# A decode block on one core: the output stored in whole rows, the MLP weights loaded in other pieces, and the second bias loaded by itself

## The chip, the cores and the metric

The kernel runs on one core of a Trainium2 chip. The metric is the device time of one execution in microseconds, the median of several runs. The core's engines work side by side: TensorE (PE, its weight loads PEld), VectorE (DVE), ScalarE (ACT), GpSimd (POOL) and SyncE (SP). SP computes nothing here; it issues the loads and the store, each a DMA that sixteen DMA engines carry out.

## The reference

Four tokens (B = 4, one per sequence) of D = 448 go through an attention block over cached keys and values, and then through an MLP, each behind a layer norm and with its residual. All is float32.

```
x = A_x                                  # 4 x 1 x 448
q = layernorm(x) @ wq                    # 16 heads of 256
k, v = the last W = 1024 rows of k_cache, v_cache   # 8 kv heads, each for 2 heads
p = softmax(q k^T / 16)
h = x + (p v) @ wo                       # wo: 4096 x 448
y = layernorm(layernorm(h))
g = gelu(y @ w1 + b1)                    # w1: 448 x 1792
out = h + g @ w2 + b2                    # w2: 1792 x 448
```

Of the 88 MB that it reads, 67 MB are k and v, 4.2 MB of each for every kv head. The four weights are 21 MB, the biases next to nothing.

## The kernel before, in words

**Tiles and loads.** `block_kernel` goes over the eight kv heads g. For each it loads one block of k with the head's part of wq behind it (`load_k`), and one of v with its part of wo (`load_v`). All large loads are issued by SP and go to a ring of four slots, taken in turn (`slot`), so a load waits until the tile that had its slot is no longer read. In order: `first` (wq of head 0 and x), k0, k1, v0, k2, v1, and so on to k7, v6. Then, in the loop's last turn (lines 310 to 320): v7 in two parts (`load_v7`, line 91), wo of heads 6 and 7 in two loads (line 314), w1 in two (line 317), w2 in three of 8, 4 and 2 chunks (line 320; a chunk is 128 rows of w2 as 128 partitions x 448, 224 KB). wo of heads 6 and 7 and w1 share a slot.

**The small rows.** x, b2 and b1 stand in one tile `rs` of 128 x 704, cleared by POOL (line 133) and filled by one ACT-issued load `rows` (line 134). With four tokens and a row of 448 cut into four quadrants there are 16 rows, and row i stands on partition 8 i (GAP = 8); the rest stays zero. `xb`, `b2b` and `b1b` are its column ranges.

**Compute.** For each head: `scores` (line 184, then maximum and exp), `project_q` for the head two ahead, `transpose_p` (line 209), `values` (line 220, po), `heads` (lines 237 to 252, po to oT) and `project_o` (line 257 into acc; for the last two heads line 263 into hsum). Behind head 7: h = hsum + x (line 352), the means and variances by small matmuls on PE (line 343), z, zT (line 368), hb = h + b2 (line 370), pu = z w1 (line 379), u with b1 and gelu (lines 392, 393), the transposes put (398, 400) and gT (402, 404), py = g w2 (line 410, eight matmuls a chunk), res = py + hb (line 414) and the store (line 415), 16 rows of 512 bytes.

**What sets the order.** PE's instructions run as the file has them. On the other engines the planner may put an instruction ahead of an earlier one that is not ready. `keep_warm(n)` puts n matmuls of zeros on PE whose results are not used; PE's clock depends on how busy it is.

The host cuts and packs the inputs, and picks the 448 columns out of the 4 x 512 that the store leaves.

Of the kernel before, what the change touches and what calls it, by code (L numbers as in the profile page):

```python
# [8 lines left out]
F32 = mybir.dt.float32  # L9
# [6 lines left out]
B, D = 4, 448  # L16
HQ, HKV, SK, DH = 16, 8, 4096, 256
REP = HQ // HKV
W = min(4096, max(256, SK // 4))
F = 1792  # L20
P = 128
# [4 lines left out]
FQ = F // 4  # L26
Q = 32
GAP = Q // B
KV = 8 * B * DH
WC = 4 * D  # L30
# [3 lines left out]
W1C = 3 * F + F // 2  # L34
# [1 line left out]
SCALE = DH ** -0.5  # L36

@with_exitstack
def block_kernel(ctx: ExitStack, tc, rows, first, kw, vw, v7, wo67, w1, w2, out):
    nc = tc.nc  # L40
    const = ctx.enter_context(tc.tile_pool(name="const", bufs=1))
    ring = ctx.enter_context(tc.tile_pool(name="ring", bufs=4))
    work = ctx.enter_context(tc.tile_pool(name="work", bufs=2))
    once = ctx.enter_context(tc.tile_pool(name="once", bufs=1))
# [3 lines left out]
    ps_m = ctx.enter_context(tc.tile_pool(name="ps_m", bufs=2, space=PSUM))  # L48
# [4 lines left out]
    def slot(name):  # L53
        return ring.tile([P, SLOT], F32, tag="t", name=name)
# [17 lines left out]
    def wo_rows(t):  # L72
        return t.rearrange("p (j e) -> p j e", j=4)

    def load_k(g):
        t = load(kw[g] if g < HKV - 1 else kw[g][:, :KV], f"k{g}")
        k = t[:, :KV].rearrange("p (h c b k) -> p h c b k", h=2, c=2, b=B)
        return [k[:, h] for h in range(2)], wq_parts(t[:, KV:]) if g < HKV - 1 else None

    def chunk_pairs(t):  # L80
        t = t.rearrange("p (c b d) -> p c b d", c=NKC, b=B)
        return [t[:, c : c + 2] for c in range(0, NKC, 2)]

    def load_v(g):
        t = load(vw[g] if g < HKV - 2 else vw[g][:, :KV], f"v{g}")
        return chunk_pairs(t[:, :KV]), wo_rows(t[:, KV:]) if g < HKV - 2 else None

    def load_v7():
        t = slot("v7")
        for a, b in ((0, V7A), (V7A, KV)):  # L90
            nc.sync.dma_start(t[:, a:b], v7[:, a:b])
        return chunk_pairs(t[:, :KV])

# [35 lines left out]
    for t in qT + oT + pT + [gT]:  # L129
        nc.gpsimd.memset(t, 0.0)  # L130

    rs = const.tile([P, 2 * P + FQ], F32, name="rs")
    nc.gpsimd.memset(rs, 0.0)
    nc.scalar.dma_start(rs[::GAP, :], rows)

    def spread(t):
        return t[..., ::GAP]
    xb, b2b, b1b = rs[:, :P], rs[:, P : 2 * P], rs[:, 2 * P :]


    def column_mean(t, name):
# [19 lines left out]
    def project_q(g, parts):  # L161
        pq = ps_m.tile([P, 512], F32, tag="m", name=f"pq{g}")
        for j, a, cols, w in parts:
            nc.tensor.matmul(pq[j * Q : (j + 1) * Q, cols], yT[:, a, :], w, start=True, stop=True)  # L164
        qs = work.tile([P, 512], F32, tag="qs", name=f"qs{g}")
        nc.scalar.copy(qs, pq)  # L166

        pt = ps_m.tile([P, 2 * REP, B], F32, tag="m", name=f"pqt{g}")
        for i in range(2 * REP):
            nc.tensor.matmul(pt[:, i, :], qs[:, i * P : (i + 1) * P], sel[:, :B], start=True, stop=True)  # L170

        src = pt.rearrange("p (r c) b -> p c b r", r=REP)
        for i in range(2):
            nc.vector.tensor_copy(qT[g % 2][:, :, :, i * REP : (i + 1) * REP], src)  # L174

    def scores(g, kt):
        s = [ps_s.tile([P, 512], F32, tag="s", name=f"s{g}_{h}") for h in range(2)]
        if g == HKV - 1:
            keep_warm(12, s[0])
        mx = work.tile([P, 2], F32, tag="mx", name=f"mx{g}")  # L180
        for h in range(2):
            for c in range(2):
                for b in range(B):
                    nc.tensor.matmul(  # L184
                        s[h][b * Q : (b + 1) * Q, :], qT[g % 2][:, c, b, :], kt[h][:, c, b, :],
                        start=(c == 0), stop=(c == 1),
                    )
            nc.vector.reduce_max(mx[:, h : h + 1], s[h], axis=AX.X)  # L188
        nm = work.tile([P, 1], F32, tag="nm", name=f"nm{g}")
        nc.vector.tensor_max(nm, mx[:, 0:1], mx[:, 1:2])  # L190
        nc.vector.tensor_scalar_mul(nm, nm, -SCALE)  # L191
        p = work.tile([P, 2 * 512], F32, tag="p", name=f"p{g}")
        sums = work.tile([P, 2], F32, tag="sums", name=f"sums{g}")
        for h in range(2):
            nc.scalar.activation(  # L195
                p[:, h * 512 : (h + 1) * 512], s[h], AF.Exp, bias=nm, scale=SCALE,
                accum_out=sums[:, h : h + 1],
            )
        rec = work.tile([P, 1], F32, tag="rec", name=f"rec{g}")
        nc.vector.tensor_add(rec, sums[:, 0:1], sums[:, 1:2])  # L200
        nc.vector.reciprocal(rec, rec)
        return p, rec

    def transpose_p(g, p):
        pt = ps_t.tile([P, NKC, P], F32, tag="t", name=f"ppt{g}")
        if g == HKV - 1:
            keep_warm(8, pt.rearrange("p c k -> p (c k)"))
        for c in range(NKC):
            nc.tensor.transpose(pt[:, c, :], p[:, c * P : (c + 1) * P], ident)  # L209

        src = pt.rearrange("p (c i) (b q) -> p c i b q", i=2, b=B)
        for i in range(2):
            nc.vector.tensor_copy(pT[g % 2][:, :, :, i * REP : (i + 1) * REP], src[:, :, i, :, :REP])  # L213
# [16 lines left out]
    def columns(t, j):  # L230
        if j < 3:
            return t[:, j * P : (j + 1) * P].rearrange("p (i c) -> p i c", i=2)
        return t[:, None, 3 * P :].to_broadcast([t.shape[0], 2, H])
# [47 lines left out]
    def keep_warm(n, to=None):  # L281
        to = tail[0][:, 0, :] if to is None else to
        for _ in range(n):
            nc.tensor.matmul(to[:Q, :512], idle[:, :Q], idle, start=True, stop=True)  # L284
# [6 lines left out]
    for g in range(HKV):  # L291
        if g + 1 < HKV:
            kt, wqt = load_k(g + 1)
            vt, wot = load_v(g)
            p, rec_next = scores(g + 1, kt)
            if g + 2 < HKV:
                project_q(g + 2, wqt)
            transpose_p(g + 1, p)
            if g + 1 == HKV - 1:
                tail.append(ps_t.tile([P, 2, 512], F32, tag="t", name="tail"))  # L300
                accs = once.tile([P, D], F32, tag="u", name="accs")
                nc.scalar.copy(accs, acc)
                keep_warm(10)
                hsum = ps_s.tile([P, 512], F32, tag="s", name="hsum")[:, :P]
                ph = hsum.rearrange("p (i c) -> p i c", i=2)
                pu = ps_s.tile([P, 512], F32, tag="s", name="pu")[:, :FQ]
                for j in range(4):
                    nc.tensor.matmul(ph[j * Q : (j + 1) * Q], sel, columns(accs, j), start=True, stop=False)
        else:
            vt = load_v7()  # L310
            tw = slot("w1")
            wo_last = [wo_rows(tw[:, i * WC : (i + 1) * WC]) for i in range(2)]
            for i in range(2):
                nc.sync.dma_start(tw[:, i * WC : (i + 1) * WC], wo67[i])
            tw1 = tw[:, 2 * WC : 2 * WC + W1C]
            for a, n in ((0, 2 * F), (2 * F, W1C - 2 * F)):
                nc.sync.dma_start(tw1[:, a : a + n], w1[:, a : a + n])
            tw2 = slot("w2")
            for c0, n in ((0, 8), (8, 4), (12, 2)):
                nc.sync.dma_start(tw2[:, c0 * D : (c0 + n) * D], w2[:, c0 * D : (c0 + n) * D])  # L320
        po = values(g, vt)
        heads(g, po, rec)
        if g < HKV - 2:
            project_o(g, wot)
        if g == HKV - 1:
            for i in range(2):
                project_o(HKV - 2 + i, wo_last[i])
        if g + 1 < HKV:
            rec = rec_next
# [20 lines left out]
    h = once.tile([P, P], F32, tag="h", name="h")  # L350
# [3 lines left out]
    m = row_mean(hs, pm[:, 0:1], "m")  # L354
# [4 lines left out]
    m = row_mean(ds, pm2[:, 0:1], "m2")  # L359
# [6 lines left out]
    pz = ps_m.tile([P, 4, B], F32, tag="m", name="pz")  # L366
    nc.tensor.matmul(pz, z, rows_of, start=True, stop=True)
    nc.vector.tensor_copy(spread(zT), pz)
    hb = once.tile([P, P], F32, tag="hb", name="hb")
    nc.vector.tensor_add(hb, h, b2b)  # L370
    keep_warm(2)

    r1 = stat("r1")
# [2 lines left out]
    for a in range(ND):  # L376
        for j in range(4):
            rows, w = w1_part(a, j)
# [27 lines left out]
    for c in range(NFC):  # L406
        for j in range(4):
            n = 2 if c == 0 or j < 3 else 1
            w = columns(w2t[c], j) if n == 2 else w2t[c][:, None, 3 * P :]
            nc.tensor.matmul(  # L410
                py[j * Q : (j + 1) * Q, :n, :], gT[:, c, :], w, start=(c == 0), stop=(c == NFC - 1),
            )
    res = once.tile([P, P], F32, tag="res", name="res")
    nc.vector.tensor_add(res, py.rearrange("p i c -> p (i c)"), hb)  # L414
    nc.sync.dma_start(out, res[::GAP, :])


# [62 lines left out]
```

## Time and profile before

| | |
|---|---|
| median of 3 runs | 215.99 us |
| the three runs | 215.67, 215.99, 216.38 us |
| the profiled execution | 215.79 us |
| its span (first to last instruction) | 213.8 us |
| mean granted clock of TensorE | 0.83 |
| read from memory | 88.29 MB, 413 GB/s over the span |
| PE, DVE, ACT, POOL busy | 71%, 16%, 11%, 3% |

The span in forty slices, of 5.3 us each:

```profile
PE   0476868294786538495957768485948897999993
DMA  7999999999999999999999999999999999999990
```

A digit is the busy share of a slice in tenths. For DMA it is the mean over the sixteen DMA engines: they are full from the first slice to the last but one. PE is busy in turns, and full only in the last slices, in which the MLP runs.

In the rows that follow, a time in front is the start in us from the span's start, the next number the duration, x32 a count. SPq is SP's queue of DMA issues, whose duration is the issuing alone. A landing time runs from the issue to the end of the transfer. A bracket at the end of a row tells how long the engine stood idle before it and for what.

### The profile page before, as it was taken

What the parts mean: (1) busy time and instruction counts of PE and PEld (TensorE: products, weight loads), DVE (VectorE), ACT (ScalarE), POOL (GpSimd) and SP (SyncE); (2) the same over time, 40 slices, a digit from 0 to 9 for tenths busy, and PEclk for the clock granted to TensorE, in tenths of its full rate; (3) what the DMA queues carried; (4) which work ended last, traced back from release to release, by engine and by line L of the source; (5) the groups of instructions that cost most, each with busy time, mean ns of one, the idle gap of its engine ahead of it and who ended that gap; (6) DMA issues with size and microseconds to landing.
All of it is one profiled execution on the core that took longest, in us unless ns stands there. A gap on an engine that the chain in (4) does not pass through costs nothing.

```text
span 213.8 us, 2594 instructions
## 1 busy us (share of the span) xinstructions
PE 151.1 (71%) x1128; PEld 63.9 (30%) x1128; DVE 33.5 (16%) x138; ACT 24.0 (11%) x57; POOL 5.6 (3%) x17
## 2 busy tenths in 40 slices
PE   0476868294786538495957768485948897999993
PEld 0342423122142213222231213122232333456352
DVE  1410313101121103100130103100220113002220
ACT  1110302000030002100030003000030102000310
POOL 6100000000000000000000000000000000000100
PEclk9999978769589959766695859666795999999999
DMA  7999999999999999999999999999999999999990
GB/s 297 412 433 441 396 478 406 427 448 403 456 421 411 478 411 426 444 396 471 418 418 448 406 456 426 411 466 418 426 419 417 460 414 411 411 418 427 428 368 22
DMA packets 3674, 88.45 MB, mean 414 GB/s; under 512 B 432, under 2 KB 448, under 8 KB 1104
## 3 DMA queue, kind: packets, MB, share of 16 engines
q1 hardware_dynamic: 3632, 88.25, 96.6%
q8 instruction: 8, 0.13, 0.3%
q10 hardware_dynamic: 32, 0.05, 0.1%
q14 instruction: 2, 0.02, 0.0%
HBM read 88.29 MB, written 0.01 MB: 413 GB/s over the span
## 4 chain that ended last, share of the span: by engine, by line
DMA 83%; PE 12%; DVE 1%; ACT 1%; SPq 1%; issue 1%; ACTq 0%
DMA v<-vw 70%; DMA w<-w 13%; PE po L220 8%; PE acc L257 2%; PE pot L245 1%; PE py L410 1%; DVE o L237 1%; ACT o L238 1%; SPq L59 0%; DVE oT L252 0%; SPq L63 0%; DVE res L414 0%; ACTq L238 0%
## 5 line engine op out<-in xcount | busy, mean ns | idle before, releaser
L184 PE MATMUL s<-k,qT 128*32 128x512 f32 x256 | 42.6, 819 | 17.4 <-DMA k<-kw 17.4
L220 PE MATMUL po<-v,pT 128*32 128x512 f32 x256 | 40.9, 792 | 18.3 <-DMA v<-vw 18.3
L184 PEld LDWEIGHTS s<-k,qT 128*32 128x32 f32 x256 | 10.4, 144 | 48.5 <-issue 28.7
L220 PEld LDWEIGHTS po<-v,pT 128*32 128x32 f32 x256 | 11.1, 140 | 42.3 <-issue 26.7
L188 DVE TENSOR_REDUCE mx<-s 128x1 f32<-128x512 f32 x16 | 11.1, 692 | 64.8 <-PE s L184 64.8
L166 ACT COPY qs<-pq 128x512 f32<-128x512 f32 x8 | 4.7, 586 | 85.8 <-PE pq L164 85.8
L170 PE MATMUL pqt<-sel,qs 128*128 128x4 f32 x64 | 9.3, 268 | 6.2 <-ACT qs L166 6.2
L245 PE MATMUL pot<-ident,o 128*128 128x8 f32 x64 | 9.8, 261 | 4.9 <-DVE o L237 3.6
L237 DVE TENSOR_SCALAR o<-po,rec 128x256 f32<-128x256 f32 x8 | 3.9, 484 | 59.9 <-PE po L220 59.9
L238 ACT ACTIVATE o<-po,rec 128x256 f32<-128x256 f32 x8 | 3.8, 474 | 72.7 <-DVE o L237 72.7
L245 PEld LDWEIGHTS pot<-ident,o 128*128 128x128 f32 x64 | 8.3, 190 | 11.7 <-DVE o L237 9.7
L195 ACT ACTIVATE p<-s,nm 128x512 f32<-128x512 f32 x16 | 10.9, 690 | 7.0 <-DVE nm L191 7.0
L170 PEld LDWEIGHTS pqt<-sel,qs 128*128 128x128 f32 x64 | 8.6, 208 | 10.4 <-ACT qs L166 10.4
L209 PE MATMUL ppt<-ident,p 128*128 128x128 f32 x64 | 9.0, 281 | 0.7 <-ACT p L195 0.7
L257 PE MATMUL acc<-v,oT 128*32 128x448 f32 x48 | 8.0, 751 | 1.7 <-DVE oT L252 1.7
L209 PEld LDWEIGHTS ppt<-ident,p 128*128 128x128 f32 x64 | 7.3, 150 | 1.7 <-ACT p L195 1.4
L164 PE MATMUL pq<-k,yT 128*32 128x512 f32 (+1 forms) x70 | 7.3, 507 | 0.0
L284 PE MATMUL tail<-idle 128*32 128x512 bf16 x26 | 7.0, 382 | 0.4 <-DVE pT L213 0.4
L284 PEld LDWEIGHTS <-idle 128*32 128x32 bf16 x52 | 4.6, 96 | 7.9 <-issue 3.9
L158 POOL TENSOR_TENSOR r<-ve_r,mhalf 128x1 f32<-128x1 f32 x2 | 1.1, 545 | 192.2 <-DVE ve_r L157 192.2
L164 PEld LDWEIGHTS pq<-k,yT 128*32 128x32 f32 x70 | 3.3, 110 | 6.0 <-issue 4.6
L174 DVE COPY qT<-pqt 128x16 f32<-128x16 f32 x16 | 2.0, 170 | 15.5 <-PE pqt L170 15.5
(97 smaller groups left out, 66.3 us busy)
## 6 DMA issues: line engine op xcount, KB each, us to landing
k<-kw SPq DMA_DIRECT2D x7, 4992.0 KB, 41.3
v<-vw SPq DMA_DIRECT2D x6, 4992.0 KB, 39.3
k<-kw SPq DMA_DIRECT2D x1, 4096.0 KB, 39.1
v<-vw SPq DMA_DIRECT2D x1, 4096.0 KB, 32.9
w<-w SPq DMA_DIRECT2D x2, 1792.0 KB, 28.7
v<-v SPq DMA_DIRECT2D x1, 3072.0 KB, 32.3
w<-wo SPq DMA_DIRECT2D x2, 896.0 KB, 22.8
w<-w SPq DMA_DIRECT2D x1, 1344.0 KB, 30.3
```

What stands on the lines that cost most here:

```text
L164: nc.tensor.matmul(pq[j * Q : (j + 1) * Q, cols], yT[:, a, :], w, start=True, stop=True)
L170: nc.tensor.matmul(pt[:, i, :], qs[:, i * P : (i + 1) * P], sel[:, :B], start=True, stop=True)
L184: nc.tensor.matmul(s[h][b * Q : (b + 1) * Q, :], qT[g % 2][:, c, b, :], kt[h][:, c, b, :], start=(c == 0), stop=(c == 1),)
L188: nc.vector.reduce_max(mx[:, h : h + 1], s[h], axis=AX.X)
L195: nc.scalar.activation(p[:, h * 512 : (h + 1) * 512], s[h], AF.Exp, bias=nm, scale=SCALE, accum_out=sums[:, h : h + 1],)
L209: nc.tensor.transpose(pt[:, c, :], p[:, c * P : (c + 1) * P], ident)
L220: nc.tensor.matmul(po[b * Q : (b + 1) * Q], pT[g % 2][:, c, b, :], vt[c][:, :, b, :], start=(c == 0), stop=(c == NKC // 2 - 1),)
L237: nc.vector.tensor_scalar_mul(o[:, 0], po[:, 0], rec)
L238: nc.scalar.mul(o[:, 1], po[:, 1], rec)
L245: nc.tensor.matmul(pt[:, c], o[:, i, c * P : (c + 1) * P], rows_of_pair[:, i * REP : (i + 1) * REP, :], start=(i == 0), stop=(i == 1),)
L257: nc.tensor.matmul(acc[i * Q : (i + 1) * Q, :], oT[g % 2][:, i, :], wt[:, i, :], start=(g == 0), stop=(g == HKV - 3),)
L284: nc.tensor.matmul(to[:Q, :512], idle[:, :Q], idle, start=True, stop=True)
```

## The change

1. The store writes the whole tile `res`, 128 rows of 512 bytes, and the host takes every eighth row.
2. b2 is no longer in `rows`. It has a tile `b2b` of 128 x 128, cleared by POOL, and eight loads on SP: for each of the four 32-column parts, the 16 rows in two loads. Parts 0 and 1 (2 and 14 rows, 6 and 10 rows) stand between v7's two loads, parts 2 and 3 (4 and 12, 8 and 8) ahead of the last load of w2. A row of a part is 128 bytes.
3. wo of heads 6 and 7 comes in one load instead of two, w1 in three instead of two, w2 in four (8, 3, 2 and 1 chunks) instead of three.
4. hb = h + b2 stands behind the matmuls of py, ahead of res; before, it stood behind zT.
5. `keep_warm(8)` is added behind `transpose_p(6, p)`, ahead of `values(5)`.

```diff
+    def load_b2(part, parted):
+        cols = slice(part * Q, (part + 1) * Q)
+        for r in (slice(0, parted), slice(parted, 4 * B)):
+            nc.sync.dma_start(b2b[::GAP, :][r, cols], b2[r, cols])
+
     def load_v7():
         t = slot("v7")
         for a, b in ((0, V7A), (V7A, KV)):
+            if a:
+                load_b2(0, 2)
+                load_b2(1, 6)
             nc.sync.dma_start(t[:, a:b], v7[:, a:b])
         return chunk_pairs(t[:, :KV])
...
-    rs = const.tile([P, 2 * P + FQ], F32, name="rs")
+    rs = const.tile([P, P + FQ], F32, name="rs")
+    b2b = const.tile([P, P], F32, name="b2b")
     nc.gpsimd.memset(rs, 0.0)
+    nc.gpsimd.memset(b2b, 0.0)
     nc.scalar.dma_start(rs[::GAP, :], rows)
...
-    xb, b2b, b1b = rs[:, :P], rs[:, P : 2 * P], rs[:, 2 * P :]
+    xb, b1b = rs[:, :P], rs[:, P:]
...
             transpose_p(g + 1, p)
+            if g + 1 == HKV - 2:
+                keep_warm(8, ps_m.tile([P, 512], F32, tag="m", name="wait"))
...
-            for i in range(2):
-                nc.sync.dma_start(tw[:, i * WC : (i + 1) * WC], wo67[i])
+            nc.sync.dma_start(tw[:, : 2 * WC], wo67)
             tw1 = tw[:, 2 * WC : 2 * WC + W1C]
-            for a, n in ((0, 2 * F), (2 * F, W1C - 2 * F)):
+            for a, n in ((0, 2 * F), (2 * F, F), (3 * F, F // 2)):
                 nc.sync.dma_start(tw1[:, a : a + n], w1[:, a : a + n])
             tw2 = slot("w2")
-            for c0, n in ((0, 8), (8, 4), (12, 2)):
+            for c0, n in ((0, 8), (8, 3), (11, 2), (13, 1)):
+                if c0 == 13:
+                    load_b2(2, 4)
+                    load_b2(3, 8)
                 nc.sync.dma_start(tw2[:, c0 * D : (c0 + n) * D], w2[:, c0 * D : (c0 + n) * D])
...
-    hb = once.tile([P, P], F32, tag="hb", name="hb")
-    nc.vector.tensor_add(hb, h, b2b)
     keep_warm(2)
...
+    hb = once.tile([P, P], F32, tag="hb", name="hb")
+    nc.vector.tensor_add(hb, h, b2b)
     res = once.tile([P, P], F32, tag="res", name="res")
     nc.vector.tensor_add(res, py.rearrange("p i c -> p (i c)"), hb)
-    nc.sync.dma_start(out, res[::GAP, :])
+    nc.sync.dma_start(out, res)
```

More of the change, by code (lines that the diff above doesn't have):

```diff
@@ L38, in block_kernel @@
 @with_exitstack
-def block_kernel(ctx: ExitStack, tc, rows, first, kw, vw, v7, wo67, w1, w2, out):
+def block_kernel(ctx: ExitStack, tc, rows, first, kw, vw, v7, wo67, w1, w2, b2, out):
     nc = tc.nc
@@ L461 @@
     b2 = np.concatenate([b2, b2[:, 3 * P :]], axis=1)
-    rows = np.concatenate([quadrants(xp), quadrants(b2), quadrants(np.asarray(B_b1).reshape(1, F))], axis=2)
+    rows = np.concatenate([quadrants(xp), quadrants(np.asarray(B_b1).reshape(1, F))], axis=2)
     rows = rows.reshape(4 * B, -1)
     arrays = {
-        "rows": rows, "first": first, "kw": kw, "vw": vw, "v7": v[-1], "wo67": wo[-2:], "w1": w1, "w2": w2,
+        "rows": rows, "first": first, "kw": kw, "vw": vw, "v7": v[-1], "wo67": np.concatenate([wo[-2], wo[-1]], axis=1), "w1": w1, "w2": w2,
+        "b2": quadrants(b2).reshape(4 * B, P),
     }
@@ L472 @@
     ]
-    out = nc.dram_tensor("out", (4 * B, P), F32, kind="ExternalOutput").ap()
+    out = nc.dram_tensor("out", (P, P), F32, kind="ExternalOutput").ap()
     with tile.TileContext(nc) as tc:
@@ L477 @@
     r = run(nc, [arrays], core_ids=[0])
-    got = np.asarray(r.results[0]["out"]).reshape(4, B, P)
+    got = np.asarray(r.results[0]["out"]).reshape(4, B, GAP, P)[:, :, 0]
     return np.ascontiguousarray(got.transpose(1, 0, 2).reshape(B, 1, 4 * P)[:, :, :D])
```

## The prediction

> **What bounds the kernel now.** I read the page's first and fourth parts, then the queue's own timeline, the DMA answers of narrow windows, and the windows of the last 4 us.
>
> ```profile
> span 213.8 us, 2594 instructions
> q1 hardware_dynamic: 3632, 88.25, 96.6%
> DMA 83%; PE 12%; DVE 1%; ACT 1%; SPq 1%; issue 1%; ACTq 0%
> 180.54 28.26 DMA w<-w
> 208.85 1.07 PE py L410 x20
> 210.00 0.68 PE py L410 x4
> 211.02 0.55 SPq L415 DMA_DIRECT2D out<-res  x1
> out<-res SPq DMA_DIRECT2D x1, 8.0 KB, 1.8
> ```
>
> One queue of loads, q1, fills 96.6% of the span, and the chain is 83% DMA. It ends in a load of w2, py, one addition (res) and a store of 8 KB. So only two things can move the end: when the last bytes of w2 land, and what must follow them.
>
> ```profile
> 155.51 0.80 SPq L91 DMA_DIRECT2D v<-v  x2
> 170.62 0.80 SPq L314 DMA_DIRECT2D w<-wo  x2
> 171.47 0.90 SPq L317 DMA_DIRECT2D w<-w  x2
> 176.64 11.55 SPq L320 DMA_DIRECT2D w<-w  x3
> v<-vw SPq DMA_DIRECT2D x1, 4096.0 KB, 32.9
> v<-v SPq DMA_DIRECT2D x1, 3072.0 KB, 32.3
> v<-v SPq DMA_DIRECT2D x1, 1024.0 KB, 34.5
> w<-wo SPq DMA_DIRECT2D x1, 896.0 KB, 23.7
> w<-w SPq DMA_DIRECT2D x1, 1792.0 KB, 27.5
> w<-w SPq DMA_DIRECT2D x1, 1344.0 KB, 30.3
> w<-w SPq DMA_DIRECT2D x1, 1792.0 KB, 29.9
> w<-w SPq DMA_DIRECT2D x1, 448.0 KB, 22.0
> SPq L320 <- DMA v<-v: 7.0, 1, 7.0
> ```
>
> Issue plus time to landing gives when each load lands. A pair's second issue is at its first's start plus about 0.4 us. The first part of v7 (the values of the last head) lands at 155.51 + 32.3 = 187.8, its second at 190.4; the second half of wo67 at 171.0 + 23.7 = 194.7; w1's two loads at 199.0 and 202.3; w2's three at 206.5, 208.8 (the chain's row: 180.54 + 28.26) and 187.9 + 22.0 = 209.9. From 202.3 to 206.5 come 1792 KB: 418 KB a us, so one of w2's fourteen chunks (224 KB) takes 0.53 us.
>
> The last row is the one on which the order hangs. L320's three loads stretch over 11.55 us because the third waits 7.0 us for v7's first part, and that is the load issued eight before it. The second is issued at 180.54, just as v6, again eight before it, lands (147.60 + 32.9 = 180.5). I read it as a rule of this program: **a load is issued only when the one eight before it has landed.** The change adds ten loads, so this must be redone.
>
> **The change part by part.**
>
> *w2 in 8, 3, 2, 1 chunks instead of 8, 4, 2.* The bytes are the same, so the last still lands near 209.9; what follows is one chunk instead of two.
>
> ```profile
> 206.70 1.71 PEld L410 LDWEIGHTS py<-w,gT 128*32 128x32 f32 x64 [0.46 <-issue]
> 206.73 1.95 PE L410 MATMUL py<-w,gT 128*32 128x128 f32 x64 [0.39 <-DVE gT L402]
> 209.97 0.40 PEld L410 LDWEIGHTS py<-w,gT 128*32 128x32 f32 x16 [0.31 <-issue]
> ```
>
> Eight chunks are 64 instructions in 1.71 us: 0.21 us a chunk. In the old kernel two chunks start at 209.97, right behind the landing at 209.9, and end at 210.68. In the new one PE goes on from 208.44 (206.73 + 8 x 0.214) without a stop: the next load has landed at 206.5 + 3 x 0.53 = 208.1, the one after at 209.2 to 209.3 (PE wants it at 209.1), and PE stands at the last chunk by 209.8. That lands at 209.9, and one chunk is saved: **-0.21 us**. Bounds: 0, if the smaller load lands 0.2 later than the pair did; -0.21 is also the most.
>
> *wo67 in one load, w1 in three.* One load of wo67 has its whole at 194.7; before, its first half could be used sooner.
>
> ```profile
> 194.42 1.86 PEld L263 LDWEIGHTS hsum<-w,oT 128*32 128x32 f32 x64
> 202.32 1.84 PE L379 MATMUL pu<-w,zT 128*32 128x448 f32 x16 [0.29 <-DMA w<-w]
> ```
>
> L263 now starts at 194.75 instead of 194.42: +0.33 on the chain of h, pm, z and pu. But in pu PE stood 0.29 us waiting for w1's second load (202.3). Split in three, its first 896 KB land at 199.0 + 2.1 = 201.1, and that wait goes. What is late next is PE itself, 0.04 us later than before; and chunk 13 of w2 waits for its landing anyway. **0.**
>
> *Eight loads of b2, and hb moved.* Four stand between v7's two parts, four before w2's last load. By the rule of eight, SP issues v7's second part when v5 lands (161.1, by the row of values(5) further down) instead of 155.9, w1's first load when v6 does (180.5), its second at 187.8, the four late b2 loads at 190.4, 194.7, 199.0 and 201.1, and w2's last at 202.3, the landing of w1's third. Behind each waiting issue stand only later loads, and each is issued 7 us or more before the stream comes to it (v7's second part 27 us; w2's last 209.4 - 202.3). The cover is the 30 us of loads already queued; without it each wait would be a gap in the stream. **0.**
>
> Their packets are not free. 64 packets of 128 bytes come into the stream, and 16 rows of the old `rows` load get shorter. The nearest row is the old store, 16 packets of 512 bytes with as many semaphore writes:
>
> ```profile
> q1 hardware_dynamic: 32, 0.01, 8.3%
> 207.50:208.00 0.50, 0.50 (x28) 0.50 (x23) 0.00 (x0) 0.00 (x0) 0.00 (x0) 1.00 0.63 251
> 208.00:208.50 0.50, 0.50 (x24) 0.41 (x15) 0.00 (x0) 0.00 (x0) 0.00 (x0) 1.00 0.56 222
> 208.50:209.00 0.50, 0.33 (x14) 0.15 (x12) 0.00 (x0) 0.00 (x0) 0.00 (x0) 1.00 0.40 158
> 209.00:209.50 0.50, 0.50 (x26) 0.50 (x22) 0.00 (x0) 0.00 (x0) 0.00 (x0) 1.00 0.17 65
> ```
>
> The first row is the DMA answer for 212.0 to 212.5: 8.3% of 16 engines in 0.5 us is 0.66 us, 0.042 us for a packet with its semaphore write. An engine that takes part in all eight loads pays at most 8 x 0.042 = 0.33 us. The windows (their last two columns are the DMA share and GB/s) show that the sixteen engines don't end together: from 208.0 on 44% of their time is already empty, 1.9 us before the last landing. So most engines have room for it. Bounds 0 (a little below, by shorter rows) to +0.33; I take **0**, since more than half of the engines end early.
>
> The Trainium skill, "DMA: Bandwidth & Descriptors", section "Why a DMA increments its semaphore by 16 and not by 1", says that such a DMA is spread over the largest k up to 16 that divides the slowest dimensions, on the lowest-numbered k engines. By it the loads of 2, 14, 6, 10, 4, 12, 8 and 8 rows put eight packets on the lowest engine and none on the two highest. No view of this trace numbers the engines, so whether the late ones are the low ones isn't shown; it is rival 3. The page's section "Rules for kernel authors" speaks against the change more plainly: transfers under 64 KB are mostly overhead and should be one. By its fixed 2 us each, eight in a row would be an estimate of 16 us. The store alone, 1.8 us for 8 KB, agrees with that figure; but the loads of w were in flight together, up to eight, and none of them shows such a pause, so I don't charge it.
>
> hb now comes after gT's copies and waits for the last b2 load, which lands before w2's last, by 209.9.
>
> ```profile
> 206.51 0.34 DVE L404 COPY gT<-put 64x8 f32<-64x8 f32 x2
> 196.97 0.29 DVE L370 TENSOR_TENSOR hb<-h,rs 128x128 f32<-128x128 f32 x1
> ```
>
> DVE is empty from 206.85 to res. hb ends at 209.9 + 0.3 = 210.2, py at 210.47; only res is queued behind it. **0**, with 0.27 us of cover; each tenth that b2 lands after 210.17 is a tenth on the path.
>
> *The store of 128 whole rows (64 KB).* A load of 128 rows issued behind a wait takes 0.33 us to issue, the old store of 16 rows 0.55:
>
> ```profile
> 147.60 0.33 SPq L59 DMA_DIRECT2D v<-vw  x1
> ```
>
> That is -0.22. Each engine then writes eight packets instead of one: 7 x 0.042 = +0.29. Sum **+0.07**; bounds -0.22 (writes overlap) and +0.29 (no shorter issue).
>
> *Eight keep_warm matmuls ahead of values(5).*
>
> ```profile
> 161.00:167.00 6.00, 5.88 (x32) 1.40 (x33) 0.00 (x0) 0.00 (x0) 0.00 (x0) 0.56 0.98 421
> 161.12 6.18 PE L220 MATMUL po<-v,pT 128*32 128x512 f32 x32 [2.90 <-DMA v<-vw]
> 183.08 3.60 PE L220 MATMUL po<-v,pT 128*32 128x512 f32 x29
> ```
>
> PE idles for 2.90 us up to 161.12, when v5 lands, and then runs the 32 matmuls of values(5) in 6.18 us; in the first row, which holds them, the granted clock is 0.56 (the third number from its end). Values(6) did 29 of its 32 in 3.60. Kept busy ahead of values(5), PE should keep its clock and end some 2 us sooner (6.18 - 3.60 x 32/29 = 2.2). Those 2 us end in the next waits for loads, v7's first part at 187.8 and wo67 at 194.7. **0**; if the clock stays low, 0 as well.
>
> **Sum:** -0.21 + 0.07 = -0.14 us, against the profiled execution's 215.79 us (the span of 213.8 and 2.0 around it): 215.65. The median of the three runs is 215.99, 0.20 above that execution; from it the sum gives 215.85. I forecast **215.8**. A difference of 0.3% (0.65 us) is about what a measurement of this kernel can tell from none.
>
> **The rivals.**
>
> 1. *The small loads are issued early, and the queue jams (slower).* The instructions of an engine do not stand in the file's order: hb, line 370, ran at 196.97, ahead of L357. The b2 loads need no free slot, only b2b's memset. Put right behind the fifth large load, the last of the eight would wait for k2, and v1 behind it.
>
> ```profile
> 2.95 0.44 SPq L59 DMA_DIRECT2D k<-kw  x1
> k<-kw SPq DMA_DIRECT2D x1, 4992.0 KB, 51.6
> first<-first SPq DMA_DIRECT2D x1, 928.0 KB, 4.6
> ```
>
> k2 lands at 2.95 + 51.6 = 54.5, when nothing else is queued; v1, which before went out while they were still under way, would be issued then. The first load took 4.6 us for 928 KB, which at 418 KB a us are 2.2, so a start from empty costs 2.4 us: 215.99 + 2.4 - 0.1 = 218.2. It decides once the jam outlasts the queued loads. For it: the moved hb. Against: SP's loads stand in the file's order all through. Chance 0.13.
>
> 2. *hb is placed ahead of gT's copies.* DVE then waits from 206.5 for b2 at about 209.4: +2.9, 218.9. In the new code it stands behind them, and b2 comes last. Chance 0.05.
>
> 3. *The packets fall on the engines that end last, and the store pays its upper bound:* -0.21 + 0.33 + 0.29 = +0.41, 216.4, still within 0.3%. Chance 0.12.
>
> 4. *The engines end more evenly (faster).* The windows' work from 207.5 on is 0.5 x (0.63 + 0.56 + 0.40 + 0.17) = 0.88 us of all sixteen. Spread evenly the stream would end 1.1 us sooner; then PE binds: 206.73 + 14 x 0.214 + 0.28 = 210.0 instead of 210.68, and the time is 215.99 - 0.68 = 215.3. Against: no bytes leave the late engines but b2's short rows. Chance 0.13.
>
> 5. *The change of w2 does nothing*, since its last load lands later by a chunk's time: 216.1. Chance 0.10.
>
> **How the numbers follow.** The forecast keeps 0.47. Within 0.3% lie the forecast, rivals 3 and 5, less a few hundredths at their edges: 0.65. Faster by more: rival 4 and a store at its low bound, 0.15. Slower: rivals 1 and 2 and the edge of 3, 0.20. The range 215.1 to 216.9 takes in the bounds of the store, the packets and the chunk (-0.43 to +0.62 on 215.99), with 0.3 us on either side for the spread of the runs, and rival 4; it leaves out 1 and 2, 0.18. The likeliest case alone spans 215.4 to 216.4.
>
> **What would show it.** Right: py's last wait is for w2's one-chunk load, with 8 instructions after it; L379 has no wait for w; the store's issue is near 0.33 us; the DMA share stays full to 207.5. Wrong: b2 loads at 3 us in the queue's timeline; a slice of low DMA share before 200 us; hb or res as the piece that waits for b2; a last w2 landing away from 209.9.

## The result, and the profile after

The changed kernel takes **215.20 us** (median of 7 runs, 215.09 to 215.72) against 215.81 us for the kernel before in the same rounds (7 runs, 215.59 to 216.38). The medians differ by 0.61 us. The ratio is 0.9969, with a 95% interval of 0.9955 to 0.9982; by it the change saves 0.67 us (0.39 to 0.97), just past the 0.3% that a measurement can tell. The forecast was 215.8 with a sum of -0.14, so the time lies within the range of 215.1 to 216.9, but 0.1 us from its low end, and below the 215.4 to 216.4 of the likeliest case. The profiled execution of the new kernel took 215.09 us, span 213.2 (before 215.79 and 213.8).

First the same parts of the page as before: the span, the queue of loads, the chain's shares by engine.

```profile
span 213.2 us, 2623 instructions
...
q1 hardware_dynamic: 4016, 88.32, 96.9%
...
DMA 80%; PE 14%; another core or an unknown queue 1%; SPq 1%; issue 0%; DVE 0%; ACT 0%
```

Nothing has changed in kind: one queue of loads fills 96.9% of the span, and the chain is DMA. The gain has to lie at the end. Next the chain of waits from 204 us on (start, us, what):

```profile
189.46 19.73 DMA w<-w
209.19 0.04 issue
209.24 0.99 PE py L422 x12
210.23 0.02 issue
210.26 0.29 DVE res L428
```

Py ends at 210.23, 0.45 us earlier than before (210.68). PE's timeline of the same stretch, and of the places the prediction spoke of (L230 are the matmuls of values, L273 those of wo67, L391 pu, L422 py; the last row is from the timeline of the weight loads):

```profile
160.90 3.64 PE L230 MATMUL po<-v,pT 128*32 128x512 f32 x32
...
194.46 1.95 PE L273 MATMUL hsum<-w,oT 128*32 128x128 f32 x64 [0.71 <-DMA w<-wo]
...
201.79 1.84 PE L391 MATMUL pu<-w,zT 128*32 128x448 f32 x16
...
206.48 2.60 PE L422 MATMUL py<-w,gT 128*32 128x128 f32 x88 [0.67 <-DMA w<-w]
209.24 0.94 PE L422 MATMUL py<-w,gT 128*32 128x128 f32 x24 [0.15 <-DMA w<-w]
209.76 0.16 PEld L422 LDWEIGHTS py<-w,gT 128*32 128x32 f32 x8 [0.16 <-DMA w<-w]
```

The last row is the last chunk: 8 weight loads that waited for DMA and began at 209.76; before, 16 began at 209.97. From that start to the end of py it now takes 0.47 us instead of 0.71. Values(5) (first row) took 3.64 us, against 6.18 in the profile before. The second part of pu (L391, before L379) has no wait for w1 in its row any more. Now SyncE's own timeline, which shows the issue of every load and the store:

```profile
156.56 0.33 SPq L99 DMA_DIRECT2D v<-v  x1
156.94 3.10 SPq L91 DMA_DIRECT2D b2b<-b  x4
160.86 0.35 SPq L99 DMA_DIRECT2D v<-v  x1
170.63 0.33 SPq L325 DMA_DIRECT2D w<-wo  x1
180.34 8.13 SPq L328 DMA_DIRECT2D w<-w  x3
188.57 1.33 SPq L334 DMA_DIRECT2D w<-w  x3
190.14 11.38 SPq L91 DMA_DIRECT2D b2b<-b  x4
202.06 0.33 SPq L334 DMA_DIRECT2D w<-w  x1
210.57 0.35 SPq L429 DMA_DIRECT2D out<-res  x1
```

The order is the one predicted: the first four loads of b2 lie behind v7's first part, v7's second part goes out at 160.86 (predicted 161.1), w1's first at 180.34 (180.5), the late loads of b2 between 190.14 and 200.9 (190.4 to 201.1), w2's last at 202.06 (202.3). The store's issue takes 0.35 us instead of 0.55. VectorE's timeline shows where the moved addition went:

```profile
209.44 0.29 DVE L426 TENSOR_TENSOR hb<-h,b2b 128x128 f32<-128x128 f32 x1 [3.11 <-DMA w<-w]
210.26 0.29 DVE L428 TENSOR_TENSOR res<-py,hb 128x128 f32<-128x128 f32 x1 [0.53 <-PE py L422]
```

It stands idle for 3.11 us, does hb at 209.44, and is free again 0.53 us before res is wanted. Last, the windows of the stream's end (us, busy time and count of PE, PEld, DVE, ACT, POOL, then the granted clock, the DMA share and GB/s):

```profile
207.50:208.00 0.50, 0.50 (x27) 0.50 (x22) 0.00 (x0) 0.00 (x0) 0.00 (x0) 1.00 0.63 238
208.00:208.50 0.50, 0.50 (x28) 0.50 (x23) 0.00 (x0) 0.00 (x0) 0.00 (x0) 1.00 0.56 213
208.50:209.00 0.50, 0.50 (x21) 0.32 (x11) 0.00 (x0) 0.00 (x0) 0.00 (x0) 1.00 0.40 148
209.00:209.50 0.50, 0.35 (x16) 0.26 (x16) 0.06 (x1) 0.00 (x0) 0.00 (x0) 1.00 0.27 79
```

The DMA shares are 0.63, 0.56, 0.40 and 0.27 (before 0.63, 0.56, 0.40 and 0.17). The sixteen engines end as unevenly as they did.

Of the 0.70 us between the two profiled executions, 0.24 is the shorter last step and 0.20 the store's issue. Another 0.2 is older than the change's last loads: the issue that waits for v6 (L328's first, before L320's second) came at 180.34 instead of 180.54. The kernels below with the same loads up to there have it anywhere from 180.27 (e5_no_warm) to 180.82 (e12_fill_gap). I take it for spread between executions.

### The profile page after: what moved, and what is told of

It is laid out like the page before. It is cut to its first block, busy times and chain, and to the rows that moved or that the text cites. A ratio compares the mean times of both kernels' runs of the same rounds, so it can differ in the third digit from the quotient of the medians.

```text
span 213.2 us, 2623 instructions
## 1 busy us (share of the span) xinstructions
PE 150.1 (70%) x1136; PEld 63.5 (30%) x1136; DVE 33.5 (16%) x138; ACT 24.0 (11%) x57; POOL 5.6 (3%) x18
## 3 DMA queue, kind: packets, MB, share of 16 engines
q1 hardware_dynamic: 4016, 88.32, 96.9%
## 4 chain that ended last, share of the span: by engine, by line
DMA 80%; PE 14%; another core or an unknown queue 1%; SPq 1%; issue 0%; DVE 0%; ACT 0%
DMA k<-kw 38%; DMA v<-vw 19%; DMA v<-v 15%; DMA w<-w 9%; PE s L194 9%; PE po L230 3%; PE pq L174 1%; PE py L422 0%; PE acc L267 0%; PE pot L255 0%; SPq L59 0%; SPq L334 0%; SPq L328 0%; DVE o L247 0%
## 5 line engine op out<-in xcount | busy, mean ns | idle before, releaser
L194 PE MATMUL s<-k,qT 128*32 128x512 f32 x256 | 46.2, 889 | 22.4 <-DMA k<-kw 22.4
L230 PE MATMUL po<-v,pT 128*32 128x512 f32 x256 | 36.0, 710 | 13.3 <-DMA v<-vw 12.2
L230 PEld LDWEIGHTS po<-v,pT 128*32 128x32 f32 x256 | 9.9, 126 | 33.9 <-issue 25.6
L294 PEld LDWEIGHTS <-idle 128*32 128x32 bf16 x60 | 5.3, 96 | 8.7 <-issue 4.0
L267 PE MATMUL acc<-v,oT 128*32 128x448 f32 x48 | 5.8, 551 | 1.7 <-DVE oT L262 1.7
```

The source lines that it names most:

```text
L194: nc.tensor.matmul(s[h][b * Q : (b + 1) * Q, :], qT[g % 2][:, c, b, :], kt[h][:, c, b, :], start=(c == 0), stop=(c == 1),)
L230: nc.tensor.matmul(po[b * Q : (b + 1) * Q], pT[g % 2][:, c, b, :], vt[c][:, :, b, :], start=(c == 0), stop=(c == NKC // 2 - 1),)
L267: nc.tensor.matmul(acc[i * Q : (i + 1) * Q, :], oT[g % 2][:, i, :], wt[:, i, :], start=(g == 0), stop=(g == HKV - 3),)
```

## The experiments

Three questions: which part brings the gain; why the store brought something where a loss of 0.07 was forecast; and what the small loads and the keep_warm matmuls cost. The first four kernels shared 31 runs of the kernel before (median 215.76), the next four 29 (215.80), the last four 24 (216.11).

**e1_store: the whole-row store alone, in the kernel before.**

```diff
-    nc.sync.dma_start(out, res[::GAP, :])
+    nc.sync.dma_start(out, res)
```

> The kernel before with only the store changed to 128 whole rows. Theory A (the gain sits behind the last load: the shorter issue is a gain and the eight packets of an engine cost nothing): the store's issue takes 0.35 us instead of 0.55, issue to landing 1.56 instead of 1.76, and the time falls by 0.20 us, ratio 0.9991. Theory B (the prediction's sum: eight packets cost 0.29 us): issue to landing 1.83, the time rises by 0.07 us, and the measured gain comes from the stream of loads.

Measured: 215.80 us, ratio 1.0002 (0.9986 to 1.0019). By the ratio, nothing. (Here and in the other kernels with another store, the size of the output and the host's slice change with it.) Its profile has the DMA answer for 210.5 to 213.2 (queue, packets, MB, share; then the issue, KB, us from issue to landing):

```profile
q8 instruction: 1, 0.02, 2.8%
...
out<-res SPq DMA_DIRECT2D x1, 64.0 KB, 2.2
```

A packet of 16 KB on the instruction queue (q8) fell into this window, and the store landed 2.2 us after its issue. 2.8% of 16 engines over 2.7 us is 1.2 us on one engine. The same answer without such a packet, from e3_b2_in_rows below, with the same store:

```profile
out<-res SPq DMA_DIRECT2D x1, 64.0 KB, 1.5
```

So 64 KB land in 1.5 us where the old 8 KB took 1.8, and e1's profiled execution (215.95) lost about 0.6, as I read it to the instruction packet: it began between 210.7 and 210.8 us, just ahead of the store's issue at 210.93; in e3 such a packet came between 209.5 and 210.0. How many of e1's 12 runs (215.43 to 217.04) lost it too isn't known. This run alone settles nothing on the store; e4 says more.

**e2_w2split: w2 in 8, 3, 2 and 1 chunks alone, in the kernel before.**

```diff
-            for c0, n in ((0, 8), (8, 4), (12, 2)):
+            for c0, n in ((0, 8), (8, 3), (11, 2), (13, 1)):
```

> The kernel before with only w2 loaded in 8, 3, 2 and 1 chunks. Theory A: the last load still lands near 209.9 us, and 0.47 us instead of 0.71 to 0.82 pass from there to the end of py: -0.25 to -0.35 us, ratio near 0.9986. Theory B (the gain comes from the small loads' place in the stream): py ends no earlier, because the one-chunk load lands later by what is saved: within 0.1 us of before.

Measured: 215.44 us, ratio 0.9988 (0.9973 to 1.0003); its lowest run is 215.21, that of the kernel before 215.50. The chain of its profile:

```profile
206.76 3.59 PE py L410 x70
210.35 0.02 issue
210.37 0.29 DVE res L414
```

Py ends at 210.35, 0.33 us earlier than before, and 0.24 and 0.26 earlier than in e1 and in e7 further down, which have the old loads (210.59, 210.61). The interval by itself just takes in no change; the profiles and the lowest runs (-0.29) agree on 0.2 to 0.3 us. It is the largest single part that was tried alone, and rival 5 (the split does nothing) doesn't hold. One more row of this profile matters later. Without the keep_warm matmuls, values(5) ran at full clock here, as it did in e1:

```profile
161.03 3.64 PE L220 MATMUL po<-v,pT 128*32 128x512 f32 x32 [1.56 <-DMA v<-vw]
```

**e3_b2_in_rows: the changed kernel, but b2 comes with the `rows` load again; the eight small loads are gone.**

```diff
-    rs = const.tile([P, P + FQ], F32, name="rs")
-    b2b = const.tile([P, P], F32, name="b2b")
+    rs = const.tile([P, 2 * P + FQ], F32, name="rs")
...
-            if a:
-                load_b2(0, 2)
-                load_b2(1, 6)
...
-                if c0 == 13:
-                    load_b2(2, 4)
-                    load_b2(3, 8)
...
```

> The changed kernel with b2 put back into the load of the small rows, no load of b2 of its own; hb stays behind py. Theory A: the small loads cost the end nothing and bring nothing; the last load of w2 lands at 209.6 to 209.9 us and the time is that of the changed kernel, ratio to the kernel before 0.997. Theory B (the small loads hold up the engines that are early and so help the late ones): the last load lands 0.15 us later than the changed kernel's 209.72, and the ratio is 0.998 or more. Theory C (their 64 packets cost something at the end): the last load lands earlier by up to 0.1 us, and the ratio is 0.9965 or less.

Measured: 215.19 us, ratio 0.9969 (0.9958 to 0.9980). With the eight loads 215.20 and 0.9969. They cost nothing and bring nothing that these runs, each known to about 0.2 us, can tell.

**e4_old_store: the changed kernel with the store of 16 rows.**

```diff
-    nc.sync.dma_start(out, res)
+    nc.sync.dma_start(out, res[::GAP, :])
```

> The changed kernel with the old store of 16 rows. Theory A: it loses 0.20 us, issue 0.55 us, issue to landing 1.76; ratio to the kernel before 0.998. Theory B: it gains 0.07 us, ratio 0.9966.

Measured: 215.37 us, ratio 0.9973 (0.9962 to 0.9984), all 11 runs between 215.23 and 215.50. That is 0.17 above the changed kernel, by two medians whose intervals overlap; the lowest runs differ by 0.14. The queue's timeline has the size in it:

```profile
210.72 0.60 SPq L429 DMA_DIRECT2D out<-res  x1
```

0.60 to issue against 0.35. By the medians and by the issue the whole-row store is worth 0.15 to 0.25 us.

**e5_no_warm: the changed kernel without the eight keep_warm matmuls.**

```diff
-            if g + 1 == HKV - 2:
-                keep_warm(8, ps_m.tile([P, 512], F32, tag="m", name="wait"))
```

> The changed kernel without the eight keep_warm matmuls ahead of values(5). Theory F (a fetch of 16 KB of instructions, due after about every 256 instructions of PE, is due at the very end; sixteen more PE instructions bring it to 209 to 210 us, ahead of the store, and without them it falls on the store): a fetch near 210.6 us, the store's issue to landing near 2.1 us instead of 1.56, runs spread over 1 us, ratio to the kernel before 0.9985 to 1.000. Theory A (the keep_warm matmuls end in later waits and do nothing): store 1.56 us, ratio 0.997.

Measured: 215.85 us, ratio 0.9985 (0.9968 to 1.0003). The runs don't stand in one heap: 215.08 to 215.31 five times, 215.81 to 216.19 seven times, with nothing between. The profile is of an upper one (215.89). Two groups of PE's timeline:

```profile
194.43 3.59 PE L273 MATMUL hsum<-w,oT 128*32 128x128 f32 x64 [0.72 <-DMA w<-wo]
...
207.83 3.26 PE L420 MATMUL py<-w,gT 128*32 128x128 f32 x112 [0.39 <-issue]
```

The 64 matmuls of wo67 (L273) took 3.59 us instead of 1.95, and everything behind them on PE is later by that, until py, which now runs through without waiting for any load: PE is what limits the end. The windows show why (the clock is the third number from the end); first this kernel, then the changed one.

```profile
194.00:196.00 2.00, 1.57 (x32) 1.46 (x36) 0.00 (x0) 0.00 (x0) 0.00 (x0) 0.60 0.96 409
196.00:198.00 2.00, 2.00 (x41) 1.75 (x34) 0.00 (x0) 0.00 (x0) 0.00 (x0) 0.54 0.98 409
```

```profile
194.00:196.00 2.00, 1.54 (x56) 1.54 (x60) 0.00 (x0) 0.00 (x0) 0.00 (x0) 1.00 0.98 416
196.00:198.00 2.00, 2.00 (x25) 1.00 (x17) 0.66 (x4) 0.22 (x2) 0.00 (x0) 1.00 0.99 416
```

The granted clock fell to half for some 3.4 us just as L273 began, behind an idle time of 0.72 us. The changed kernel idles as long there (0.71) and kept its clock. Py ends at 211.12 instead of 210.23: 0.89 late, and the two heaps lie about 0.8 apart.

**e6_b2_early: rival 1 made on purpose. All eight loads of b2 go out right behind k2.**

```diff
-            if a:
-                load_b2(0, 2)
-                load_b2(1, 6)
...
             kt, wqt = load_k(g + 1)
+            if g == 1:
+                for part, parted in ((0, 2), (1, 6), (2, 4), (3, 8)):
+                    load_b2(part, parted)
             vt, wot = load_v(g)
...
-                if c0 == 13:
-                    load_b2(2, 4)
-                    load_b2(3, 8)
```

> The changed kernel with all eight b2 loads issued right behind k2. If a load is issued only when the one eight before it has landed: the eighth b2 load goes out when k2 lands (54.0 us), v1 only then (24.2 us in the changed kernel), the DMA share falls to nothing for about 2 us near 54, the last load of w2 lands near 212, and the ratio to the kernel before is 1.007. If there is no such rule: v1 at 24.2, ratio 0.997.

Measured: 219.77 us, ratio 1.0183 (1.0165 to 1.0202). The queue's timeline, and the windows from 52 us on:

```profile
4.10 50.82 SPq L91 DMA_DIRECT2D b2b<-b  x8
55.05 0.36 SPq L59 DMA_DIRECT2D v<-vw  x1
```

```profile
52.00:54.00 2.00, 0.64 (x5) 0.00 (x0) 0.00 (x0) 0.00 (x0) 0.00 (x0) 0.50 0.08 22
54.00:56.00 2.00, 1.63 (x8) 0.40 (x12) 0.00 (x0) 0.00 (x0) 0.00 (x0) 0.50 0.05 9
```

The eight small loads hold the queue from 4.10 to 54.92 us. V1, which goes out at 24.22 in the changed kernel, goes out at 55.05, and for four microseconds the DMA share is 0.08 and 0.05. The rule of eight holds, and breaking its cover costs 4.6 us over the changed kernel, not the 2.4 that rival 1 had: I had counted one start from empty, and by these windows the engines ran nearly dry from 52 us on, some 3 us before v1 went out.

**e7_warm_only and e8_store_warm: the kernel before with the eight keep_warm matmuls (the cut), and with these and the whole-row store of e1.**

```diff
             transpose_p(g + 1, p)
+            if g + 1 == HKV - 2:
+                keep_warm(8, ps_m.tile([P, 512], F32, tag="m", name="wait"))
```

> The kernel before with only the eight keep_warm matmuls. Theory F: the fetch moves from the end to 209.5 to 210.5 us; what runs of the kernel before lie above 216 us go, and the median falls by 0.1 to 0.2 us, ratio 0.9992. Theory A: nothing, ratio 1.000, with the same spread. If a faster values(5) reached the end, the last load of w2 or py would end earlier, by up to 2 us.

> The kernel before with the store of whole rows and the eight keep_warm matmuls, but the old loads. Theory F: what the store alone did not bring (ratio 1.0002, its landing 2.17 us because a fetch fell on it) comes now: fetch before 210.5, store 1.56 us, ratio 0.9982 to 0.999. Theory B (the whole-row store brings nothing by itself): ratio 1.000.

Measured: e7 215.92 us, ratio 1.0007 (0.9993 to 1.0022); e8 215.44, ratio 0.9985 (0.9974 to 0.9996). Alone the matmuls bring nothing. With the store they go with -0.32 us, a little more than the store's own 0.15 to 0.25. In e8's profile the DMA answer for 210.5 to 213.2 has no row of the instruction queue, and the store landed after 1.6 us:

```profile
out<-res SPq DMA_DIRECT2D x1, 64.0 KB, 1.6
```

That left two theories for what the matmuls do: they shift the instruction queue's packets away from the store, or they change when PE's clock falls. E5's upper execution speaks for the second: SyncE waited 1.2 us for its store to land, as in the changed kernel, against 1.8 in e1. The next run tells them apart.

**e9_warm_at_head1: the same eight matmuls, moved ahead of values(0).** The count of instructions stays; the place is some 120 us earlier.

```diff
-            if g + 1 == HKV - 2:
+            if g + 1 == 1:
                 keep_warm(8, ps_m.tile([P, 512], F32, tag="m", name="wait"))
```

> The changed kernel with the eight keep_warm matmuls moved from ahead of values(5) to ahead of values(0), some 120 us earlier: the same number of PE instructions, without their effect on PE's clock near 160 us. Without them (no_warm) 7 of 12 runs stood at 215.8 to 216.2 us and 5 at 215.1 to 215.3. Theory F (the count of PE instructions sets when the last fetch falls): as the changed kernel, no second group, median 215.2, ratio 0.997. Theory G (without the eight at that place PE's granted clock falls to 0.5 for 3.4 us near 194 us in some runs, as in the profile of no_warm): two groups again, median 215.3 to 215.9, ratio 0.9975 to 0.9995.

Measured: 215.99 us, ratio 0.9978 (0.9960 to 0.9996), again two heaps: 215.07 to 215.22 five times, 215.94 to 216.16 seven times. The profile is of an upper one (216.08):

```profile
194.63 3.49 PE L273 MATMUL hsum<-w,oT 128*32 128x128 f32 x64 [0.72 <-DMA w<-wo]
...
207.93 3.26 PE L422 MATMUL py<-w,gT 128*32 128x128 f32 x112 [0.39 <-issue]
```

The same picture as in e5: it is the place of the matmuls that matters, not their number, and what goes with the upper profiles is the low clock at 194 us.

**e10_store64: the changed kernel, with every second row stored** (64 rows, 32 KB).

```diff
-    nc.sync.dma_start(out, res)
+    nc.sync.dma_start(out, res[::2, :])
```

> The changed kernel with every second row of res stored, 64 rows. If the issue time goes by the number of rows, it is between 0.35 us (128 rows) and 0.55 to 0.60 (16 rows), about 0.45; if a step between rows sets it, 0.55 to 0.60; if any multiple of 16 with 4 or more rows an engine is quick, 0.35. Issue to landing in the first case 1.6 us.

Measured: 215.49 us in its one run. The queue's timeline:

```profile
210.72 0.55 SPq L429 DMA_DIRECT2D out<-res  x1
```

64 rows with a step between them take 0.55 us to issue, as 16 rows do (0.55 to 0.60); 128 without a step take 0.35. In these profiles it goes with the step between the rows, not with their number.

**e11_best and e12_fill_gap: attempts at a better version.** E12 is e5 with four keep_warm matmuls instead of one in heads(7), to fill the idle time ahead of L273. E11 is e3 with that, and w2's last chunk in two loads of 256 and 192 columns. The first cut is in both, the second in e11 alone.

```diff
-            keep_warm(1)
+            keep_warm(4 if g == HKV - 1 else 1)
```

```diff
-                nc.sync.dma_start(tw2[:, c0 * D : (c0 + n) * D], w2[:, c0 * D : (c0 + n) * D])
+                for a, b in ((0, n * D),) if n > 1 else ((0, 2 * P), (2 * P, D)):
+                    nc.sync.dma_start(tw2[:, c0 * D + a : c0 * D + b], w2[:, c0 * D + a : c0 * D + b])
```

> The changed kernel with b2 in the load of the small rows, w2's last chunk loaded in two parts (256 and 192 columns) and the three keep_warm matmuls in heads(7). 4 of the last chunk's 8 matmuls are left behind the last landing: 0.1 us sooner than the changed kernel's lower runs (215.1), 215.0, ratio 0.996, if the last part lands no later; 215.2, ratio 0.997, if the smaller packets give it back.

> The kernel no_warm (the changed kernel without the eight keep_warm matmuls ahead of values(5)) with three more in heads(7), in the 0.7 us in which PE waits for wo67. Theory G: PE's clock has no reason to fall at 194 us, the group at 215.8 to 216.2 is gone, median 215.1 to 215.25, ratio 0.9968. Theory F: three matmuls are six instructions, the fetch comes 0.1 us sooner, and both groups stay, ratio 0.9985.

Measured: e12 215.14 us, ratio 0.9962 (0.9944 to 0.9979), five of seven runs from 215.07 to 215.19 and two at 215.61 and 215.77; e11 215.52, ratio 0.9972 (0.9959 to 0.9985), five runs from 215.09 to 215.18 and seven from 215.50 to 215.76. Neither beats the changed kernel. In e11's profile (215.75) the clock is low in values(7):

```profile
187.80 5.34 PE L220 MATMUL po<-v,pT 128*32 128x512 f32 x32 [1.03 <-DMA v<-v]
...
207.67 3.26 PE L410 MATMUL py<-w,gT 128*32 128x128 f32 x112 [0.39 <-issue]
```

5.34 us instead of 3.64, behind another idle time of 1.03 us; the matmuls of wo67 start later, and py runs through from 207.67. E3, which has the eight matmuls but no fillers, has the same 5.34 us in its profile (215.36), and there py ends at 210.51, against 210.23 in the changed kernel and 210.96 in e11: where PE is late, three fillers cost it another 0.45 us.

E12's profiled execution is one of its two upper ones (215.61), and it differs from e5's:

```profile
161.40 6.41 PE L230 MATMUL po<-v,pT 128*32 128x512 f32 x32 [2.67 <-DMA v<-vw]
...
207.52 3.26 PE L420 MATMUL py<-w,gT 128*32 128x128 f32 x112 [0.39 <-issue]
```

Values(5) ran at half clock, the clock at 194 us is full, and PE is late all the same. The loads are late here too: v5, for which values(5) waits, landed 0.5 us later than in the changed kernel (161.40 against 160.90). So an upper run doesn't always mean a low clock at 194 us.

## Why the prediction came out as it did

- **w2 in four loads: right, a little small.** Predicted -0.21, and as the most; in the pair of profiles the last step takes 0.24 us less, and e2 alone has py 0.24 to 0.33 earlier.
- **wo67 in one load, w1 in three: the sum of 0 held, by other numbers.** In the pair of profiles L273 started at 194.46, not 194.75, so almost nothing of the 0.33 was lost. But in the profile before PE was late there from its slow values(5): in e1, e2 and e7, with the old loads and values(5) in 3.64 us, the same matmuls started at 193.46 to 193.48 and pu at 199.06 to 199.07, against 199.35 in the changed kernel, so the single load costs 0.3 us at that place. The last part of pu started at 201.79 instead of 202.32 (202.21 to 202.24 in e1, e2 and e7), so 0.4 to 0.5 came back rather than 0.29. PE was therefore not late at py: it waited 0.67 us there for w2's first load. That wait hides the gain. I didn't try the two splits alone.
- **Eight loads of b2, hb moved: right.** Every issue time came within 0.3 us, no window ran empty, hb held nothing up, and e3 gives the same time without the loads. On the Trainium skill, "DMA: Bandwidth & Descriptors", section "Rules for kernel authors", which counts transfers under 64 KB as mostly overhead: eight of 0.2 to 1.8 KB inside a full stream cost nothing here that can be told (215.20 against 215.19), as the prediction had read from the overlapping loads of w. In e6 what cost 4.6 us was the order of the queue.
- **The store: the mis-sized term.** Predicted +0.07 as "-0.22" for the issue and "7 x 0.042 = +0.29" for seven more packets an engine. The issue was right (0.20 shorter). The packets cost nothing that can be seen: 64 KB landed in 1.5 to 1.6 us from the issue, 8 KB in 1.8. The 0.042 us came from a window with one packet and one semaphore write on an engine; I charged the sum of both to each further packet. The lower of the two bounds was the answer, -0.2.
- **keep_warm: the step that failed.** The clock of values(5) came out as said, and the 2.5 us ended in the next waits. The pair of profiles alone doesn't show that the matmuls did it, since e1 and e2 had full clock there without them. All the profiles together do: values(5) took 3.64 us in all eight with the matmuls at that place, and in the six without 3.64 twice and 4.94 to 6.41 four times. The nearest pair is the kernel before and e7, that kernel with the eight matmuls, since their clocks step at the same place. First the window of the kernel before in which values(5) begins, then that of e7 (the clock is again the third number from the end, 0.50 and 1.00):

```profile
159.46:162.88 3.42, 1.76 (x12) 0.44 (x16) 0.00 (x0) 0.00 (x0) 0.00 (x0) 0.50 0.98 422
```

```profile
159.48:162.90 3.42, 2.43 (x23) 0.70 (x25) 0.00 (x0) 0.00 (x0) 0.00 (x0) 1.00 1.05 450
```

  But "if the clock stays low, 0 as well" looked only at values(5). Without the eight matmuls at that place, seven of twelve runs lie 0.8 to 0.9 us higher (e5, and e9 with the matmuls elsewhere); with them, at most one in seven of the changed kernel (215.72), none in eleven of e4 and none in seven of e3. The cover that I named, the waits for loads, is spent at 194 us: in the changed kernel PE has 0.67 us of room before w2's first load, and 3.4 us of half clock in L273 cost 1.64. The matmuls don't keep the clock up to the end, either: it fell in values(7) in four of the eight profiles with them (e3, e6, e8, e11), where most of the loss ends in later waits (1.70 us in values(7), 0.28 at py's end in e3). E11 has the matmuls and a second heap of its own, 0.3 to 0.7 us up; in the one profiled, the fillers' 0.45 are part of it.
- **The rivals.** 1 didn't happen, and e6 shows that its mechanism is real. 2 and 3 didn't happen: hb came last on DVE, and neither packets nor store cost anything. 4 (engines that end evenly) didn't either, though the time is near its 215.3: the shares of the last windows are all but unchanged. 5 is refuted by e2 and by the last chunk's start in the changed kernel. A slip in 1 changes nothing: 215.99 + 2.4 - 0.1 is 218.3, not 218.2.

Summed by what the runs gave, -0.24 to -0.33 for w2 and -0.15 to -0.25 for the store make -0.4 to -0.6. The lowest runs of the two kernels differ by 0.50 (215.09 against 215.59). The 0.67 of the ratio has both within its interval.

That the time fell into the range is in part luck. The bounds of the terms and the 0.3 us for spread end at 215.26; the range went down to 215.1 for rival 4, which didn't come. A gain of more than 0.3% had a chance of 0.15, by rival 4 or a store at its low bound. It came by the store and by a chunk of w2 a little over its bound, and the change was three to five times the -0.14 of the sum.

**What stays open.** Why eight matmuls at 160 us change how often the clock falls at 194. PE does the same from 187.8 to 194.4 us in e5 as in the changed kernel (values(7) 3.64 us in both), so it isn't what PE does just ahead; and the clock steps at other places in each execution (last section), and no execution with the matmuls was profiled in which it steps at 194.4. Only upper executions of e5 and e9 were profiled, so that all seven upper runs of each have the same cause is inferred from their distance; e12's profile shows that it needn't be.

The runs above 216 us of e1 and of the kernel before have more than one cause. An instruction packet on the store was seen once. Of the seven such runs of the kernel before among the 31 that e1 to e4 shared, three have a long span (214.5 to 214.8 us), and four have a span of 213.7 to 213.8 like the quickest, and lose 2.8 to 3.0 us outside it instead of the usual 1.8. Of all runs whose span is on record, 25 of 132 with the old loads of wo67 and w1 (the kernel before, e1, e2, e7, e8) have 2.1 to 3.0 us outside the span, and none of 73 with the new ones (1.7 to 1.9). So a small part of the gain lies outside the span, where the profile shows nothing, and no run tells which piece of the change brings it.

## What to carry to other kernels

At the end of a kernel that is bound by its loads, shrink what follows the last landing: the last load's own work (one chunk less, 0.2 to 0.3 us) and the store's issue (whole rows instead of a stepped slice, 0.2 us, although eight times the bytes are written). Small loads cost nothing that could be told inside a full stream, as long as the queue didn't stop at them, so count which load each one waits for. And a step costed at nothing because a later wait absorbs it needs a second look at the next stretch without such a wait, in more than one execution: the clock there may differ from run to run.

## What the runs showed of the hardware

- The issue of a DMA by SyncE took 0.33 to 0.35 us for 128 whole rows behind a wait, 0.55 to 0.60 for 16 or 64 rows with a step, and 0.59 to 0.83 for the loads of 2 to 14 short rows, the last by this group of the changed kernel (lowest, median and highest ns of one, then from when to when):

```profile
L91 SPq DMA_DIRECT2D b2b<-b x8: 587/698/830, 156.9 to 200.9; - x8
```

- An instruction packet takes time of the sixteen DMA engines: one of 16 KB took 1.2 us of one engine, and the store that followed it landed 0.6 to 0.7 us later than in e8 and e3 (e1, seen once).
- The granted clock was either full or half, and in all fourteen traces it held each for a multiple of 3.41 us. Where the steps stood in the span differed between executions: it fell at 194.42 us in e5 and e9 (the windows above, 0.60 and 0.54, are 3.41 us of half clock), at 188.15 to 188.72 in e3, e8 and e11, at 159.46 in the kernel before.
- The fall at 194.42 came behind an idle time of 0.72 us. The Trainium skill, "TensorE: Matmul & The Clock Gate", section 'Part 1: The HAM clock gate (the "warmup" mystery)', says that PE falls to half after at least one idle window of about 3.4 us. The length agrees. These traces do not agree with an idle time of that length: from 185 us on none stands ahead of L273 in e5 or e9, and in the 3.41 us before the fall PE was busy for 2.32 us in e5 and 2.51 in e9. Nor does the busy time alone decide it: e1 had 1.82 us in the window from 158.60 to 162.02, and its clock didn't fall.
